# The fourth chunk's second layer of batches 1 to 6 as seven block products, with the weight sums on GpSimd

## The chip, the cores and the metric

The kernel runs on one core of a Trainium2 chip. The metric is device time in microseconds (us) of one execution. Engine names: PE is the matrix engine, DVE the vector engine, ACT the scalar engine, POOL is GpSimd. In the lines shown, `ps` is PSUM, the memory in which PE's products land and which DVE and ACT empty (an eviction); the other tiles named here lie in SBUF. The granted clock is the share of its full rate that PE was given. Times below are medians of unprofiled runs; spans, waits and instruction times come from one profiled run of each kernel.

## The reference

Eight batches of 2496 rows by 256 columns. Each is Fourier-transformed along its rows, mixed by a complex weight, soft-thresholded, and transformed back. The result goes through one of eight experts, chosen by the batch's mean: a first layer 256 to 1024 with ReLU, and a second layer 1024 to 256.

```python
X = np.fft.rfft(x, axis=1)
Yr = Xr @ w_r - Xi @ w_i + b_r
Yi = Xr @ w_i + Xi @ w_r + b_i
Yr = np.sign(Yr) * np.maximum(np.abs(Yr) - lam, 0.0)   # the same for Yi
y = np.fft.irfft(Y, n=x.shape[1], axis=1)
# experts, x being y from here on:
e_idx = np.argmax(logits, axis=1)
h = np.maximum(x[mask] @ w1[e], 0.0)
out[mask] = gate_w[mask, None, None] * (h @ w2[e])
```

## The kernel before

A Python list scheduler places every operation: each is declared with an engine, an assumed duration, a wanted time, its dependencies and the buffers it allocates and releases. Batch b's expert work is interleaved with batch b+1's transforms (towards its end, with the first of batch b+2's), so that PE always has something to do. The transforms come in groups (q). The code below is of one group. The soft threshold is a clip on DVE (`cl`) followed by four subtractions `Y = z - cl`, each with both inputs in SBUF; the inverse transform on PE waits for them.

```python
def cl_(_, cell=cell):
    nc.vector.tensor_scalar(out=cell["cl"], in0=cell["z"], scalar1=-LAM, scalar2=LAM,
                            op0=ALU.max, op1=ALU.min)
...
def y_(_, cell=cell):
    for r in range(2):
        for i in range(2):
            s = slice(64 * i, 64 * i + 64)
            nc.vector.tensor_sub(out=Y[64 * r : 64 * r + 64, :, i],
                                 in0=cell["z"][s, r], in1=cell["cl"][s, r])
...
m = S.mm([256] * n, mmv, vt, deps=[oy, t_in[4 * q + 3]], ...)   # inverse, needs Y
```

The second layer of a chunk of 512 rows normally takes eight groups of four matmuls of 256 columns. In the last batch its first four chunks use seven products of half-size blocks instead of eight, a fast form in the manner of Strassen and Winograd. It needs sums of weight blocks (tile `T`, one buffer, four subtractions of 512 elements) and sums of activations (tile `S`). A batch's `T` can be written only when the previous holder's products have released it.

```python
FAST = {(B - 1, c) for c in range(4)}
...
def add_weight_sums(b, w, wk, v):
    tk = S.tok("T", 1)                       # one buffer
    def ts(_):
        ...
        sub = nc.vector.tensor_sub
        sub(out=T[:, 0], in0=w2[:, 0, 1], in1=w2[:, 0, 0])
        ...                                  # T1, T2, T3
    t = S.op("DVE", 1.4, ts, v, deps=[w], lat=1.5, allocs=[tk])
...
# in add_fast
p5 = prod(2.4, ("F", 1), "S1", T(0), False, [o1, t_op], after=p2)
...
t_tok.rel += [p4, p5, p6, p7]                # T is free after these
```

## Time and profile before

| | before |
|---|---|
| time, 3 runs | 431.3 us (431.11 to 431.45) |
| span of the profiled run | 429.5 us |
| second-layer matmuls (L1438), product matmuls (L1252) | 1056, 224 |
| from one batch's second-layer weight load to the next | 49.97 us |
| mean granted PE clock | 1.000 |

The period is (350.02 - 200.12)/3, from the starts of the loads in GpSimd's timeline. The prediction below shows the head of the page and PE's timeline. The lines here are those that the result has to be held against. First, from the slices of the page, the PE clock that was granted, one digit for each fortieth of the span (9 is 90% or more):

```profile
PEclk9999999999999999999999999999999999999999
```

The clock is never cut.

### The profile page before, as it was taken

What the parts mean: (1) busy time and instruction counts of PE and PEld (TensorE: products, weight loads), DVE (VectorE), ACT (ScalarE), POOL (GpSimd) and SP (SyncE); (2) the same over time, 40 slices, a digit from 0 to 9 for tenths busy, and PEclk for the clock granted to TensorE, in tenths of its full rate; (3) what the DMA queues carried; (4) which work ended last, traced back from release to release, by engine and by line L of the source; (5) the groups of instructions that cost most, each with busy time, mean ns of one, the idle gap of its engine ahead of it and who ended that gap; (6) DMA issues with size and microseconds to landing.
All of it is one profiled execution on the core that took longest, in us unless ns stands there. A gap on an engine that the chain in (4) does not pass through costs nothing.

```text
span 429.5 us, 9604 instructions
## 1 busy us (share of the span) xinstructions
PE 417.4 (97%) x3601; PEld 315.9 (74%) x3601; DVE 305.3 (71%) x635; ACT 336.1 (78%) x654; POOL 60.6 (14%) x104
## 2 busy tenths in 40 slices
PE   5988999999999999999999999999999999999996
PEld 2557777887777877778677876778777787777775
DVE  1697865777777797787967787677977878414561
ACT  3789888787967887779866798678877788778884
POOL 5553100001003020033000320031200030001000
PEclk9999999999999999999999999999999999999999
DMA  7999797929885996889885998959978276521222
GB/s 151 234 172 163 129 279 238 216 75 181 230 270 106 232 186 195 251 171 203 191 247 194 197 203 209 283 117 218 194 220 253 86 166 126 181 91 56 65 99 92
DMA packets 71847, 76.98 MB, mean 179 GB/s; under 512 B 7128, under 2 KB 45744, under 8 KB 71800
## 3 DMA queue, kind: packets, MB, share of 16 engines
q1 hardware_dynamic: 58834, 56.23, 44.7%
q0 software_dynamic: 12704, 19.88, 29.1%
q8 instruction: 28, 0.46, 0.4%
q10 hardware_dynamic: 262, 0.25, 0.2%
q14 instruction: 19, 0.16, 0.1%
HBM read 57.54 MB, written 37.49 MB: 221 GB/s over the span
## 4 chain that ended last, share of the span: by engine, by line
PE 92%; DVE 3%; DMA 2%; ACT 2%; POOL 1%; issue 1%; SPq 0%; DVEq 0%; POOLq 0%
PE ps L1389 31%; PE ps L1438 27%; PE ps L914 9%; PE ps L718 4%; PE ps L547 4%; PE ps L812 3%; PE ps L1058 3%; PE ps L1252 3%; PE ps L876 3%; PE ps L1323 2%; DMA xin<-in_x_dram 1%; PE ps L751 1%; PE ps L754 1%; DMA ysb<-in_w_i_dram 1%; DVE z L766 1%; ACT ysb L1074 1%
## 5 line engine op out<-in xcount | busy, mean ns | idle before, releaser
L1402 ACT ACTIVATE hs<-ps 128x512 f16<-128x512 f32 (+3 forms) x313 | 172.1, 568 | 65.3 <-PE ps L1389 61.3
L1389 PE MATMUL ps<-ysb,w1s 128*128 128x512 f16 (+3 forms) x688 | 182.6, 359 | 0.1
L1438 PE MATMUL ps<-w2s,hs 128*128 128x256 f16 x1056 | 150.9, 272 | 0.0
L1438 PEld LDWEIGHTS <-hs 128*128 128x128 f16 x1056 | 102.0, 98 | 38.3 <-issue 0.9
L1389 PEld LDWEIGHTS <-w1s 128*128 128x128 f16 x688 | 73.9, 113 | 17.9 <-issue 0.7
L956 DVE TENSOR_TENSOR Y<-z,cl 64x512 f16<-64x512 f16 x120 | 50.4, 420 | 2.7
L928 DVE TENSOR_TENSOR tt<-ps,bias 128x512 f16<-128x512 f32 x60 | 38.6, 686 | 18.1 <-PE ps L914 17.9
L914 PE MATMUL ps<-w,XT 128*128 128x256 f16 x360 | 49.9, 273 | 0.1
L914 PEld LDWEIGHTS <-XT 128*128 128x128 f16 x360 | 34.9, 98 | 9.9 <-DVE XT L895 0.6
L1455 ACT ACTIVATE ost<-ps,gbc 128x512 f32<-128x512 f32 (+1 forms) x57 | 38.4, 675 | 2.7 <-PE ps L1438 1.9
L937 DVE TENSOR_TENSOR z<-ps,tt 128x512 f16<-128x512 f32 x60 | 38.7, 683 | 0.2
L1074 DVE CAST ysb<-ps 128x468 f16<-128x468 f32 (+1 forms) x37 | 21.4, 587 | 22.7 <-PE ps L1058 20.0
L554 ACT CAST V<-ps 128x512 f16<-128x512 f32 x52 | 30.2, 598 | 0.6
L822 ACT CAST A<-ps 120x512 f16<-120x512 f32 x46 | 26.0, 613 | 3.1 <-PE ps L812 3.1
L884 ACT CAST XT<-ps 128x512 f16<-128x512 f32 x41 | 24.3, 596 | 0.0
L1074 ACT CAST ysb<-ps 128x468 f16<-128x468 f32 (+1 forms) x47 | 21.8, 533 | 2.4 <-PE ps L1058 2.4
L1150 POOL DMA_DIRECT2D w1s<-in_moe_w_dram x8 | 6.0, 755 | 122.3 <-PE ps L1058 111.6
L547 PE MATMUL ps<-Y,ti 128*128 128x256 f16 x140 | 23.0, 272 | 0.0
L884 DVE CAST XT<-ps 128x512 f16<-128x512 f32 x19 | 13.1, 689 | 13.8 <-PE ps L876 13.0
L812 PE MATMUL ps<-xin,wa 117*120 117x512 f16 x66 | 22.8, 380 | 0.1
L1404 DVE TENSOR_SCALAR hs<-ps 128x512 f16<-128x512 f32 (+3 forms) x31 | 17.4, 568 | 7.3 <-PE ps L1389 6.5
L1058 PE MATMUL ps<-wi,V 120*128 120x117 f16 (+1 forms) x308 | 22.5, 213 | 0.0
(112 smaller groups left out, 476.5 us busy)
## 6 DMA issues: line engine op xcount, KB each, us to landing
out_dram<-ost SPq DMA_DIRECT2D x71, 256.0 KB
scr<-V SPq DMA_DIRECT2D x35, 256.0 KB
xin<-in_x_dram POOLq DMA_DIRECT2D x21, 390.0 KB, 9.8
XB<-fwd SPq DMA_DIRECT2D x30, 256.0 KB
V<-scr SPq DMA_DIRECT2D x14, 504.0 KB
fwd<-A SPq DMA_DIRECT2D x18, 360.0 KB
w1s<-in_moe_w_dram POOLq DMA_DIRECT2D x8, 512.0 KB, 7.1
w2s<-in_moe_w_dram POOLq DMA_DIRECT2D x8, 512.0 KB, 8.1
```

The costliest lines, as they stand in the source:

```text
L547: nc.tensor.matmul(pv[:, D * i : D * i + D], ti[:, 4 * q + k, :], cell["Y"](k))
L812: nc.tensor.matmul(pa[0:120, :], wa, xin_t[b][:, xcol(2 * gp) : xcol(2 * gp) + 2 * D])
L884: COPY[eng](out=cell["X"][:, ch, :, 0:2].rearrange("p a r i k -> p a i r k"), in_=hc["p"].rearrange("p (a i r k) -> p a i r k", a=2, i=2, ...
L914: nc.tensor.matmul(pm[:, D * a : D * a + D], cell["X"][:, ch, a, t].rearrange("p i k -> p (i k)"), w4[:, ch, t, :], start=(ch == 0), stop= ...
L928: nc.vector.tensor_add(out=cell["tt"][:, r], in0=cell["T", 2].rearrange("p (a c) -> p a c", a=2), in1=bias[:, r].unsqueeze(1).to_broadcast ...
L937: nc.vector.tensor_add(out=cell["z"][:, r], in0=cell["T", 1 - r].rearrange("p (a c) -> p a c", a=2), in1=cell["tt"][:, r])
L956: nc.vector.tensor_sub(out=Y[64 * r : 64 * r + 64, :, i], in0=cell["z"][s, r], in1=cell["cl"][s, r])
L1074: COPY[eng](out=yv[:, :, 12 * gb : 12 * gb + 3 * nf].rearrange("p a (g j) -> p a g j", j=3), in_=pi[:, 0 : 117 * nf].rearrange("p (g a j) ...
L1389: nc.tensor.matmul(ph[:, 0:nl], w1v[:, ch, fc // 4, :, fc % 4], ysb_t[b][:, ch, ns : ns + nl], start=(ch == 0), stop=(ch == 1))
L1402: nc.scalar.activation(out=o, in_=i, func=AFT.Relu)
L1438: nc.tensor.matmul(oc["p"][:, i, :], cell["hs"][:, ft, ts], w2s_t[b][:, ft, :], start=(ft == 0), stop=(ft == E - 1))
L1455: nc.scalar.activation(out=ost[:, 0:n], in_=oc["p"][:, 0:n], func=AFT.Copy, scale=gbc_t[b])
```

## The change

Its intent is to remove PE work, since PE sets the time: the fourth chunk of batches 1 to 6 also gets the seven products. Their weight sums go to GpSimd, which is mostly idle. Two smaller edits apply to all fast chunks: the first product waits for four of the eight activations only, and output rows are dealt to partitions in adjacent pairs.

```diff
-    FAST = {(B - 1, c) for c in range(4)}
+    FAST = {(B - 1, c) for c in range(4)} | {(b, c) for b in range(1, B - 1) for c in (3,)}
...
-            sub = nc.vector.tensor_sub
+            sub = (nc.gpsimd if b < B - 1 else nc.vector).tensor_sub
...
-        t = S.op("DVE", 1.4, ts, v, deps=[w], lat=1.5, allocs=[tk])
+        p = b < B - 1
+        t = S.op("POOL" if p else "DVE", 4.5 if p else 1.4, ts, v, deps=[w],
+                 lat=4.7 if p else 1.5, allocs=[tk])
...
-        A = {"11": lambda f, t: cell["hs"][:, f, m * t : m * t + m],
+        A = {"11": lambda f, t: cell["hs"][:, f, t:th:2],
...  (the other six operands alike)
-        p1 = prod(0, ("E", 0), "11", w2(0, 0), True, h_ops, [ek])
+        p1 = prod(0, ("E", 0), "11", w2(0, 0), True, h_ops[:4], [ek])
...
-                        "(i p) c -> p i c", p=m),
+                        "(p i) c -> p i c", i=2),
```

More of the change, by code (lines that the diff above doesn't have):

```diff
@@ L1234, in add_fast @@
         o4 = s_op("s4", 0, s4, vt(0.3), [o2])
-        A = {"11": lambda f, t: cell["hs"][:, f, m * t : m * t + m],
-             "12": lambda f, t: cell["hs"][:, 4 + f, m * t : m * t + m],
-             "22": lambda f, t: cell["hs"][:, 4 + f, th + m * t : th + m * t + m],
-             "S3": lambda f, t: cell["hs"][:, f, th + m * t : th + m * t + m],
-             "S1": lambda f, t: fc["S"][:, 0, f, m * t : m * t + m],
-             "S2": lambda f, t: fc["S"][:, 1, f, m * t : m * t + m],
-             "S4": lambda f, t: fc["S"][:, 2, f, m * t : m * t + m]}
+        A = {"11": lambda f, t: cell["hs"][:, f, t:th:2],
+             "12": lambda f, t: cell["hs"][:, 4 + f, t:th:2],
+             "22": lambda f, t: cell["hs"][:, 4 + f, th + t : nl : 2],
+             "S3": lambda f, t: cell["hs"][:, f, th + t : nl : 2],
+             "S1": lambda f, t: fc["S"][:, 0, f, t:th:2],
+             "S2": lambda f, t: fc["S"][:, 1, f, t:th:2],
+             "S4": lambda f, t: fc["S"][:, 2, f, t:th:2]}
         w2 = lambda k, h: lambda f: w2s_t[b][:, 4 * k + f, P * h : P * h + P]
```

## The prediction

> **What bounds the kernel now.** I read the head of the page first, then the chain that ended last.
>
> ```profile
> span 429.5 us, 9604 instructions
> PE 417.4 (97%) x3601; PEld 315.9 (74%) x3601; DVE 305.3 (71%) x635; ACT 336.1 (78%) x654; POOL 60.6 (14%) x104
> ...
> PE 92%; DVE 3%; DMA 2%; ACT 2%; POOL 1%; issue 1%; SPq 0%; DVEq 0%; POOLq 0%
> ```
>
> The matrix engine (PE) is busy 97% of the span, and the chain runs through it for 92%. In the list of waits, PE's own add up to under 9 us, all of them in the start-up. So a microsecond of PE work removed in the middle is a microsecond off the end, unless another engine becomes late. Busy does not mean full rate, so next come the start times of consecutive PE groups, first in the middle of the kernel (second layer L1438, first layer L1389), then in the last batch, which already uses seven products (L1252):
>
> ```profile
> 221.46 0.60 PE L1438 MATMUL ps<-w2s,hs 128*128 128x256 f16 x4
> 221.89 0.59 PE L1389 MATMUL ps<-ysb,w1s 128*128 128x512 f16 x2
> 222.33 0.60 PE L1438 MATMUL ps<-w2s,hs 128*128 128x256 f16 x4
> ...
> 404.59 0.61 PE L1252 MATMUL ps<-T,S 128*128 128x128 f16 x8
> 405.03 0.59 PE L1389 MATMUL ps<-ysb,w1s 128*128 128x512 f16 x2
> 405.46 0.61 PE L1252 MATMUL ps<-T,S 128*128 128x128 f16 x8
> ```
>
> The first column is the start. Four matmuls of 256 columns take 0.435 us of issue time (109 ns each), two of 512 take 0.435, and one block product (8 of 128 columns) takes 0.44 us (55 ns each). Weight loads (98 ns each in the groups) lie beside the matmuls and do not limit either. Multiplying the period's matmuls by these spacings (first layer 16.8 us, second 17.0, the six transform groups 15.7) gives about 49.5 us, and a batch takes 49.5 to 50: the stream has hardly a hole, no more than about 0.4 us a batch.
>
> The two engines that empty PSUM have room on average. Stretches of one batch (columns: length, PE, PE weight loads, DVE, ACT, POOL):
>
> ```profile
> 219.00:229.00 10.00, 10.00 (x81) 7.46 (x79) 7.26 (x14) 6.07 (x12) 0.00 (x0) 1.00 0.89 270
> 229.00:239.00 10.00, 10.00 (x85) 7.62 (x83) 7.98 (x22) 6.97 (x14) 3.77 (x7) 1.00 0.51 133
> 239.00:249.00 10.00, 10.00 (x112) 8.57 (x110) 8.36 (x16) 8.31 (x17) 0.80 (x2) 1.00 1.07 210
> 249.00:259.00 10.00, 10.00 (x82) 7.29 (x80) 8.15 (x16) 8.40 (x19) 3.03 (x5) 1.00 1.04 203
> ```
>
> The fourth chunk's second layer is issued at 236.7 to 243.8 us here, so its new work falls where DVE and ACT are already at 8.4 and 8.3 of 10.
>
> **What the Trainium skill says.** (1) "TensorE: Matmul & The Clock Gate", Back-to-back issue gap: it gives about 81 ns per matmul for sustained weight-load and matmul pairs of 128 columns, and 56 ns as the isolated gap. By the first figure seven products would cost 56 x 81 = 4.5 us (an estimate from that page), more than the eight they replace. The trace disagrees: 55 ns, each with its own weight load. I use the trace. (2) "GPSIMD Engine Reference", section 3.1: a two-input elementwise operation costs GpSimd about 2.6 cycles an element, twice DVE. The kernel before has no such instruction on GpSimd; its one-input operations of 128x512 took 0.78 and 1.50 us, against 0.29 us on DVE, which does not contradict it. (3) "SBUF — State Buffer", Who interferes with whom: a DVE instruction with two SBUF inputs and a GpSimd instruction that reads SBUF exclude each other for their whole length. No part of the trace before overlaps the two, so it cannot confirm this. (4) "VectorE: DVE Perf Modes", the perf-mode tier table: two-input 16-bit operations run at two elements a cycle, from PSUM at one. The trace agrees: the sums of 1024 fp16 elements took 684 to 692 ns, the additions of 512 fp32 from PSUM 683 ns.
>
> **The change part by part.**
>
> PE, per batch 1 to 6. Removed: 32 matmuls of 256 columns, 8 groups of four at 0.435 us, 3.48 us. Added: 56 of 128 columns, 7 products at 0.44 to 0.447 us (the chain has three in a row in 1.34 us), 3.08 to 3.13 us. Saved 0.35 to 0.40, say 0.38 us. All of it is on the path. Six batches: 2.3 us.
>
> DVE and ACT, per batch. Added on DVE: four sums of activations, 4 x 0.685 = 2.74 us, and three scaled additions of 256 columns at 0.482, 1.45 us. Added on either: four scaled copies of 256 columns, 4 x 0.483 = 1.93 on ACT. Removed from either: two evictions of 512 columns, 2 x 0.686 = 1.37. Net +4.75 us on the pair, whose load is 78.2 of 2 x 50 us, so 83 of 99 afterwards. Beside PE on average. Locally it is tight: from 236 to 250 us the pair is busy 10.5 + 11.5 = 22.0 of 28 us, and with 4.75 more it is 26.7, 95%.
>
> GpSimd, per batch 1 to 6: four subtractions of 512 elements. With 2.6 cycles at 1.2 GHz each is 1.1 us plus dispatch, so 1.2 to 1.5 us and 5 to 6 us in all (an estimate from the GPSIMD page and the 1.50 us row). GpSimd is 14% busy. The sums are needed a long way into a batch (the third product of the fourth chunk), while the weights land some 8 us after their issue at about 250 us, far ahead. The one tile for the sums is held until the previous batch's fourth chunk is done, so I expect them to run just after it, around the next weight issue: off the path. During those 5 to 6 us the two-SBUF-input DVE work (2.1 us per transform group of about 10 us) can be blocked, at a guess two instructions by 0.6 us, about 1 us of DVE time.
>
> Last batch: its four chunks already use the products. The first product may start after four instead of eight activations, but PE is gapless there (chunk starts follow first-layer groups with no hole), so I give it 0 to 0.2 us. Output rows become adjacent pairs, which makes longer runs per store; stores are not on the path there (DMA share 0.26), and the final piece of the kernel is still the unchanged fifth chunk. 0.
>
> Sum: 431.3 - 2.3 - 0.1 = 428.9 us if nothing becomes late.
>
> **The rivals.**
>
> A, evictions become late. In the fast form both accumulator banks are held for the whole chunk, and one half bank passes through four copies: product, copy, product, copy. Each turn is 0.44 us of product, about 0.5 of copy and the queue of ACT, so PE needs other work between the products; at 95% local load of DVE and ACT this work itself may wait for a bank. Against: in the last batch ACT takes just these copies and PE has no hole; and before, PE waits for nobody after the start, with transforms of the next batch as filler. The transform data has slack: the loads that hold GpSimd's next input load are complete at 235.2, the inverse that uses such data starts at 244.2. For: the casts at 244.6 to 249.0 must end before the next batch's first layer at 249.96, about 1 us of slack. If PE loses 0.2 us a batch, the result is 428.9 + 1.2 = 430.1; if 0.6 us, 432.5.
>
> B, GpSimd. If the sums block DVE's turn at a bad moment or push the loads of inputs and weights on the same queue, each costs up to about 1 us. For: they lie beside the same crowded stretch. Against: the weight load is a full batch ahead. It would make 429.5 to 432.
>
> C, the products run at the page's 81 ns. Then each batch loses 4.5 - 3.48 = 1.0 us, 437 us in all. The last batch's own trace speaks against it.
>
> D, the whole static order is remade by the kernel's list scheduler, so small holes can come or go anywhere: some +-0.7 us.
>
> **Range and chances.** Full gain 428.9; I charge 0.15 us a batch, 0.9 us, for A and B together, as the local load is near saturation: 429.8 us. The low end is the full gain with a favourable reordering, 428.3; the high end has PE losing about 0.5 us a batch, 432.0. Faster by over 2% means below 422.7, beyond anything that 2.3 us of removed PE time can give: 0.01. Slower by over 2% means above 439.9, for which C and A would have to meet: 0.015. Within 2%: 0.975.
>
> **What would show it.** Right: matmuls at L1438 fall from 1056 to 864 and those of the product line rise from 224 to 560, with product spacing near 0.44 us in batches 1 to 6; PE's waits stay near zero after the start; ACT and DVE together gain about 28 us; four GpSimd subtractions per batch of 1.2 to 1.5 us each, with the next weight load following without delay. A wrong size of the gain would show in products at over 0.46 us. Rival A would show as idle PE before first-layer or product matmuls released by ACT or DVE at the end of each batch, rival B as two-input DVE rows well over 0.42 us beside GpSimd's. The prediction fails if those holes exceed 0.5 us a batch, or if the reordering moves the transforms of the next batch so that the first layer waits at a batch's start.

## More of the kernel before

```profile
244.20 0.37 PE L1058 MATMUL ps<-wi,V 120*128 120x117 f16 x4
244.41 0.60 PE L547 MATMUL ps<-Y,ti 128*128 128x256 f16 x4
...
248.11 0.83 PE L1323 MATMUL ps<-hs,w2s 128*128 128x192 f16 x8
```

The subtractions end at 244.23. The inverse (L547) follows its predecessor on PE 0.21 us after that one's start, with no wait marked in brackets. It starts only 0.18 us after Y is complete: Y has next to no slack in this order.

The costliest-groups view (count, then busy us and mean ns, then idle us before them): the 120 threshold subtractions take 420 ns each.

```profile
L956 DVE TENSOR_TENSOR Y<-z,cl 64x512 f16<-64x512 f16 x120 | 50.4, 420 | 2.7
```

Then DVE's and PE's timelines of the same group of a batch (start, busy us, engine, line, operation, count):

```profile
242.49 1.74 DVE L956 TENSOR_TENSOR Y<-z,cl 64x512 f16<-64x512 f16 x4
```

## The result

| | before | after |
|---|---|---|
| time, 4 runs each | 431.38 us (431.11 to 431.87) | 453.55 us (452.11 to 455.02) |
| span of the profiled run | 429.5 us | 450.7 us |
| product / second-layer matmuls | 224 / 1056 | 560 / 864 |
| mean granted PE clock | 1.000 | 0.985 |

The ratio is 1.0513, with a 95% interval of 1.0468 to 1.0558: 5% slower. A ratio here is the mean time of one kernel's fast runs over that of the other's of the same rounds, so not quite the ratio of the medians quoted.

Head, slices and chain of the changed kernel's page:

```profile
span 450.7 us, 9985 instructions
...
PE 422.8 (94%) x3745; PEld 320.9 (71%) x3745; DVE 334.3 (74%) x664; ACT 341.9 (76%) x679; POOL 90.7 (20%) x128
...
PEclk9999999999999899998999989999999989999999
...
PE 84%; DVE 9%; DMA 2%; issue 2%; ACT 1%; POOL 0%; DVEq 0%; SPq 0%; POOLq 0%
```

PE's share of the chain fell from 92 to 84%, DVE's rose from 3 to 9%, and four slices have a lowered clock. PE is busy longer although it has less to do. The list of waits (us in total, times, longest) names what it waits for, and what starts GpSimd's sums:

```profile
POOL T L1193 <- PE ps L1254: 64.9, 5, 40.2
...
PE ps L547 <- DVE Y L956: 14.9, 10, 2.0
```

This second wait did not exist before. The group in question, with the same 120 instructions:

```profile
L956 DVE TENSOR_TENSOR Y<-z,cl 64x512 f16<-64x512 f16 x120 | 67.4, 561 | 2.7
```

The mean of 561 ns hides two kinds. Five times, four instructions take 1.28 us each and the others 0.42. One of the five, on GpSimd, DVE and PE:

```profile
253.65 1.34 POOL L1193 TENSOR_TENSOR T<-w2s 128x512 f16<-128x512 f16 x1 [5.23 <-PE ps L1254]
...
257.54 1.32 POOL L1196 TENSOR_TENSOR T<-w2s,T 128x512 f16<-128x512 f16 x1
```

```profile
254.01 5.13 DVE L956 TENSOR_TENSOR Y<-z,cl 64x512 f16<-64x512 f16 x4
```

```profile
255.57 0.37 PE L1058 MATMUL ps<-wi,V 120*128 120x117 f16 x4
257.90 0.27 PE L547 MATMUL ps<-Y,ti 128*128 128x256 f16 x1 [1.96 <-DVE Y L956]
259.19 0.49 PE L547 MATMUL ps<-Y,ti 128*128 128x256 f16 x3 [1.02 <-DVE Y L956]
...
260.91 1.45 PE L1325 MATMUL ps<-hs,w2s 128*128 128x192 f16 x8
```

The sums of batch b start as soon as the products of batch b-1 release `T`. Within 0.4 us DVE begins the threshold of batch b+1. Four GpSimd subtractions and four DVE subtractions run over the same 5.2 us, and each DVE one takes 1.28 us, about as long as a GpSimd one, instead of 0.42. PE runs out of other work and waits 1.96 us and then 1.02 us for Y. And after it has its data, eight matmuls at L1325 take 1.45 us where before they took 0.83. The windows view (columns: stretch, length, PE, PE weight loads, DVE, ACT, POOL, clock, DMA share, GB/s) shows why:

```profile
255.00:260.00 5.00, 2.02 (x22) 1.59 (x21) 4.91 (x6) 0.83 (x3) 4.52 (x4) 1.00 0.27 74
260.00:265.00 5.00, 5.00 (x45) 4.42 (x43) 1.76 (x5) 3.58 (x9) 0.63 (x1) 0.66 0.90 138
```

PE is busy 2.0 of 5 us in the first window, and in the next the clock granted is 0.66. That is a mean over 5 us: in windows of 1 us the clock is 0.50 from 260.40 to 263.81 and 1.00 around it. This happened after four of the five waits, each time for 3.41 us, so each cost 1.7 us.

The traces also show why not after the fifth. The four cuts start at 151.17, 205.78, 260.40 and 366.21 us, which is 16, 16 and 31 times 3.413 us apart, as if the clock were decided on a fixed grid of that step. Divide the trace by this grid and add up, cell by cell, the time in which PE issued nothing: it is 2.10 to 3.01 of 3.41 us in the cells just before the four cuts, and at most 1.96 in the cells of the wait that no cut followed. All ten cuts within PE's work in the profiled runs last 3.41 us and follow a cell with 2.10 us or more (sums_after_y: 2.28 to 2.58); of the cells from 40 us on that no cut follows, one has as much (2.10, sums_after_ysb). That is a rule worked out from these traces alone, and no run was made to test it. By it, the same two waits cost 1.7 us of clock or nothing, depending on where in the grid they fall.

**Where 21.2 us of span went.** The waits are 14.9. The wait counted is a little shorter than the hole: the group at 255.57 needs 0.21 us to issue (its like before: 244.20 to 244.41), so PE issued nothing for 257.90 - 255.78 = 2.12 us, 0.16 more than counted. Ten such: 1.6. The clock: (1 - 0.985) x 450.7 = 6.8, which is also four times 1.7. (The other three runs had clocks of 0.979 to 0.983, so they may have lost up to some 9.5 us.) Less 2.3 for the products: 14.9 + 1.6 + 6.8 - 2.3 = 21.0.

### The profile page after: what moved, and what is told of

Its sections match the earlier page's. It is cut to its first block, busy times and chain, and to the rows that moved or that the text cites. A ratio compares the mean times of both kernels' runs of the same rounds, so it can differ in the third digit from the quotient of the medians.

```text
span 450.7 us, 9985 instructions
## 1 busy us (share of the span) xinstructions
PE 422.8 (94%) x3745; PEld 320.9 (71%) x3745; DVE 334.3 (74%) x664; ACT 341.9 (76%) x679; POOL 90.7 (20%) x128
## 4 chain that ended last, share of the span: by engine, by line
PE 84%; DVE 9%; DMA 2%; issue 2%; ACT 1%; POOL 0%; DVEq 0%; SPq 0%; POOLq 0%
PE ps L1391 29%; PE ps L1440 20%; PE ps L914 9%; PE ps L1254 5%; DVE Y L956 5%; PE ps L547 4%; PE ps L718 4%; PE ps L812 3%; PE ps L1058 3%; PE ps L876 3%; PE ps L1325 2%; DMA xin<-in_x_dram 1%; DVE z L937 1%; PE ps L751 1%; PE ps L754 1%
## 5 line engine op out<-in xcount | busy, mean ns | idle before, releaser
L1404 ACT ACTIVATE hs<-ps 128x512 f16<-128x512 f32 (+3 forms) x317 | 177.5, 580 | 52.6 <-PE ps L1391 49.7
L1440 PE MATMUL ps<-w2s,hs 128*128 128x256 f16 x864 | 123.4, 273 | 0.0
L1440 PEld LDWEIGHTS <-hs 128*128 128x128 f16 x864 | 83.7, 98 | 30.9 <-issue 0.9
L956 DVE TENSOR_TENSOR Y<-z,cl 64x512 f16<-64x512 f16 x120 | 67.4, 561 | 2.7
L1074 ACT CAST ysb<-ps 128x468 f16<-128x468 f32 (+1 forms) x63 | 33.5, 564 | 9.7 <-PE ps L1058 9.6
L554 ACT CAST V<-ps 128x512 f16<-128x512 f32 x47 | 27.8, 601 | 16.8 <-PE ps L547 16.3
L547 PE MATMUL ps<-Y,ti 128*128 128x256 f16 x140 | 24.1, 275 | 14.9 <-DVE Y L956 14.9
L1457 ACT ACTIVATE ost<-ps,gbc 128x512 f32<-128x512 f32 (+1 forms) x45 | 30.2, 672 | 3.0 <-PE ps L1440 1.9
L547 PEld LDWEIGHTS <-ti 128*128 128x128 f16 x140 | 13.2, 98 | 22.0 <-issue 16.4
L1058 PE MATMUL ps<-wi,V 120*128 120x117 f16 (+1 forms) x308 | 26.6, 225 | 0.0
L1254 PEld LDWEIGHTS <-hs 128*128 128x128 f16 x320 | 20.9, 98 | 6.3 <-ACT ost L1269 1.2
L1058 PEld LDWEIGHTS <-V 120*128 120x128 f16 x308 | 22.1, 104 | 2.8
```

Of the source, the lines that this page charges most:

```text
L547: nc.tensor.matmul(pv[:, D * i : D * i + D], ti[:, 4 * q + k, :], cell["Y"](k))
L956: nc.vector.tensor_sub(out=Y[64 * r : 64 * r + 64, :, i], in0=cell["z"][s, r], in1=cell["cl"][s, r])
L1058: nc.tensor.matmul(pi[:, 117 * i : 117 * i + M], V2[:, g, ch * P : ch * P + P], w)
L1074: COPY[eng](out=yv[:, :, 12 * gb : 12 * gb + 3 * nf].rearrange("p a (g j) -> p a g j", j=3), in_=pi[:, 0 : 117 * nf].rearrange("p (g a j) ...
L1254: nc.tensor.matmul(fc[dst[0]][0:m, dst[1], t, :], A[a](f, t), bb(f), start=start and t == 0 and f == 0, stop=f == 3, skip_group_check=True)
L1404: nc.scalar.activation(out=o, in_=i, func=AFT.Relu)
```

## The experiments

**Theory H (hold).** GpSimd's subtractions hold DVE's two-input subtractions back, instruction by instruction; PE waits for Y; its idleness lowers the clock. **Rivals:** A, the evictions are late, or the remade order is at fault (D); or GpSimd, being busy, delays the loads that it issues; or the row and first-product edits cost something; or the waits and the clock are independent, the clock being cut for another reason. Unless told otherwise, a kernel's result was correct, and its edit is against the changed kernel. "Order kept" means that each engine's instruction order is as in the changed kernel. The expectations call H "theory L", A and D together "rival S" (or S2), and the delayed loads "rival P".

### The sums without reads

GpSimd fills `T` with zeros instead of subtracting: same place and order, no SBUF input. The result is wrong, as in m2_half and m0_later.

```diff
-            sub(out=T[:, 0], in0=w2[:, 0, 1], in1=w2[:, 0, 0])
+            nc.gpsimd.memset(T[:, 0:2], 0.0) if b < B - 1 else sub(out=T[:, 0], in0=w2[:, 0, 1], in1=w2[:, 0, 0])
...  (the other three alike, on 2:4, 0:2 and 2:4)
```

> Wrong result on purpose: the four subtractions on GpSimd of batches 1 to 6 become four zero fills of twice as many elements, so that GpSimd is about as long at work in the same places (about 1.2 us each) but reads nothing. The order on PE, DVE, ACT and the DMA queue is unchanged, row for row. Theory L (DVE's subtractions with two SBUF inputs wait for GpSimd's, PE waits for DVE, and PE's clock is cut after that wait): the Y subtractions are back at 0.42 us, PE waits for none of them, clock 1.00, 428.5 to 430.5 us. Rival S (the remade order or the chain of copies in the fast chunk costs the time): stays above 445. Rival P (GpSimd's occupancy delays its weight loads): stays above 445 too, since GpSimd is as busy.

Measured 434.85 us (433.31 to 436.47), ratio 1.0076. Y was back at 0.42 us, and no wait for L956 was left: the subtractions cause the hold, and neither the order, which was kept, nor the evictions, nor GpSimd's being busy. That it is their reading, and not something else in which a subtraction differs from a fill, is argued and not shown: no run had GpSimd read in another way. But the time was 5.6 us above the full gain, for a reason I had not thought of. Fills need no weights, so batch 1's ran at 52 us already, where the changed kernel's sums still wait for the weight load (they run at 60.9). There DVE was due to do another kind of instruction, the clip of a threshold (L779), which has one input:

```profile
51.87 4.53 DVE L779 TENSOR_SCALAR cl<-z 128x1024 f16<-128x1024 f16 x1
```

```profile
55.14 0.98 POOL L1196 MEMSET T<- 128x1024 f16 x1
```

```profile
57.18 0.39 PE L547 MATMUL ps<-Y,ti 128*128 128x256 f16 x2 [3.86 <-DVE Y L781]
```

The clip took 4.53 us; the kernel before has it at 0.43. It ended only after the last of the four fills, which ran back to back from 52.47 to 56.12. PE waited 3.86 us, and the clock fell again (0.50 for 3.41 us, 1.7 us lost). So the experiment had brought a hold of its own, once. The next one leaves batch 1 as it is (its sums meet nothing in the changed kernel, at 1.15 to 1.16 us each):

```diff
-            ... if b < B - 1 else sub(...)
+            ... if 1 < b < B - 1 else sub(...)
```

> Wrong result on purpose: as the run with zero fills, but batch 1 keeps its real subtractions, since there the fills met DVE's clip of 1024 elements (4.53 us instead of 0.47) and PE waited 3.9 us; zero fills only in batches 2 to 6. The order is that of the changed kernel. Theory L: nothing holds DVE now, no wait of PE after the start, clock 1.00, a batch takes 49.5 us instead of 50.0; 428.6 to 429.6 us, which is the gain that the seven products were forecast to bring. Rival S2 (a part of the loss is not the exclusion but comes with the remade order): 431 us or more.

Measured 429.83 us (428.94 to 430.07), ratio 0.9959 (0.9946 to 0.9973), clock 1.000, no wait for Y. A batch takes 49.55 us against 49.97 before. That is 0.42 us gained by the products in each batch, and all 22 us of the loss gone, by replacing only five batches' sums with fills.

### Half of the sums

The first two subtractions real, the last two fills.

> Wrong result on purpose: the first two subtractions on GpSimd stay, the last two become zero fills of about the same length; the order everywhere is that of the changed kernel. Theory L: two of the four Y subtractions of one transform group per batch are held by about 0.87 us each instead of four, so DVE is 1.7 us late instead of 3.4, PE waits about 1.3 us a batch instead of 3.0; with five batches 6.5 us plus a smaller loss of clock: 435 to 444 us. Rivals S and P: no change, above 450.

```diff
-            sub(out=T[:, 2], in0=w2[:, 1, 1], in1=w2[:, 0, 1])
-            sub(out=T[:, 3], in0=w2[:, 1, 0], in1=T[:, 1])
+            nc.gpsimd.memset(T[:, 2:4], 0.0) if b < B - 1 else sub(...)   # twice
```

Measured 437.07 us (436.75 to 437.82), ratio 1.0131, clock 1.000.

```profile
PE ps L547 <- DVE Y L956: 6.5, 10, 1.1
```

The waits are dosed by the number of reading instructions: two holds fewer take (14.9 - 6.5)/5 = 1.7 us of counted wait from each batch, which is two times 1.28 - 0.42. And waits of 1.10 and 0.19 us leave the clock at 1.000: PE issued nothing for at most 1.62 us in any stretch of 3.41.

### The clock by itself

Nine matmuls on constant data fill the first wait of PE, without changing Y or the sums. If the clock is cut because PE idles, it comes back; if not, nothing changes.

```diff
-                                   if wide else bank(tv))
+                                   if wide else bank(tv)); [nc.tensor.matmul(pv, warm[:, 0:P], warm) for _ in range(9 if b > 2 and q == 1 and u == 0 else 0)]
```

> Right result: the changed kernel with nine dummy matmuls of 512 columns (1.94 us) put before the inverse product that waits for the held Y, in the five batches where it waits; they go into the bank which that product overwrites. All else is in the same order. Theory: the exclusion costs the wait (about 3.0 us a batch, which stays, 1.96 of it now filled), and the cut clock afterwards (6.8 us in the profiled run) comes from PE having stood idle: clock 1.00 and 446 to 448 us, and less spread between runs. If the cut clock has another cause: 452 to 456 us and clock 0.98.

Measured 445.93 us (445.68 to 446.96), ratio 1.0343, a little better than expected. While PE works the clock is 1.000; the 0.998 comes from a cut after PE's last matmul (440.8 us), which costs nothing.

```profile
252.87 2.11 PE L544 MATMUL ps<-warm 128*128 128x512 f16 x9
255.00 0.27 PE L547 MATMUL ps<-Y,ti 128*128 128x256 f16 x1
256.29 0.49 PE L547 MATMUL ps<-Y,ti 128*128 128x256 f16 x3 [1.02 <-DVE Y L956]
```

The useless matmuls gained 7.6 us over the changed kernel. Y still took 562 ns in the mean, and the second wait of 1.02 us stayed. So the clock's share is a consequence of PE's idleness, and real. The 7.6 us, a difference of medians, are not the clock alone: five holes fewer, at 0.16 us of issue each, make 0.8 of them. The rest agrees with the 6.8 read from the trace.

### The other parts of the change

First the sums back on DVE (the order is remade), then none of the products, only the first product's half and the row pairs in the last batch.

```diff
-            sub = (nc.gpsimd if b < B - 1 else nc.vector).tensor_sub
+            sub = nc.vector.tensor_sub
-        p = b < B - 1
+        p = False
```

> Right result: the weight sums of batches 1 to 6 go to DVE, as those of the last batch do; all else as changed (the list scheduler remakes the order). Theory L: the seven products gain their 2.3 us, DVE takes 1.7 us more a batch: 428.5 to 431 us, no wait of PE after the start, clock 1.00. Rival S: above 440, as the fast chunk and its chain of copies are all there.

Measured 432.25 us (431.68 to 433.24), ratio 1.0016 (1.0003 to 1.003), somewhat above what I had expected. Y was back at 419 ns and the clock at 1.000. But PE had new small waits, the largest of them for scaled additions on DVE (1.5 us in four) and for activations (0.7 in three). The holes eat the gain: rival A or D, which this run cannot tell apart, exists at some 3 us in this form, though not as the cause of the 22.

```diff
-    FAST = {(B - 1, c) for c in range(4)} | {(b, c) for b in range(1, B - 1) for c in (3,)}
+    FAST = {(B - 1, c) for c in range(4)}
```

> Right result: only the small parts of the change (first product after four activations, alternate rows per tile and so paired output rows) in the last batch; batches 1 to 6 as before, no sums on GpSimd. All theories: within 0.5 us of before, 430.9 to 431.8 us.

Measured 431.38 us (431.21 to 432.1), ratio 1.0002 (0.9989 to 1.0016): worth nothing, as predicted.

With the sums on DVE, I also tried the products in the second or the third chunk, where DVE and ACT might have more room:

```diff
-    FAST = ... for c in (3,)}
+    FAST = ... for c in (1,)}          # dve_chunk2; (2,) in dve_chunk3
```

> Right result: weight sums on DVE, and the seven products in the second chunk of batches 1 to 6 instead of the fourth, where before DVE and ACT were busy 7.3 and 6.1 of 10 us. If what the sums-on-DVE kernel lost was the local load of DVE and ACT in the fourth chunk: 428.8 to 430.8 us. If the fast chunk's own chain of copies costs PE the same anywhere: 431.5 to 433 us.

> Right result: the same with the third chunk. Local load theory: 429 to 431.3 us, between the second and the fourth chunk. Chain of copies: 431.5 to 433 us.

Measured 431.1 us (430.58 to 431.89), ratio 0.9991 (0.9965 to 1.0018), and 430.76 us (430.44 to 431.21), ratio 0.9981 (0.9956 to 1.0007). Neither is told apart from before: both intervals hold 1. In the second chunk PE had a hole of 0.3 us ahead of the last of the seven products in each batch. Placing the sums on DVE is safe but gives the gain back in small holes.

### Moving the sums in time

If the collision is one of time, sums on GpSimd that come after Y must keep the gain. Two tries through the scheduler:

```diff
-        t_tok.rel += [p4, p5, p6, p7]
+        t_tok.rel += [p4, p5, p6, p7, a12]     # sums_after_y
```

```diff
-        ... ts, v, deps=[w],
+        ... ts, v, deps=[w] + y_ops,           # sums_after_ysb
```

> Right result: the tile of weight sums is released one step later, after the last scaled addition of the fast chunk, which stands behind the four Y subtractions in DVE's queue, so GpSimd's subtractions come after them and meet DVE's copies from PSUM instead. The list scheduler remakes parts of the order. Theory L: the Y subtractions take 0.42 us, PE does not wait for them: 428.6 to 431 us. If the exclusion also holds for copies from PSUM or the subtractions meet another two-input DVE operation: 433 to 445 us.

> Right result: GpSimd's sums wait until the batch's own input (ysb) is complete, about 8 us later than in the changed kernel, beside the sums of transformed halves (L895) and the next group's chain. Theory L: better than the changed kernel, but a two-input DVE operation or two a batch can still be held by up to 1.3 us each, where PE follows closely behind: 429 to 436 us.

Both missed. The first gave 448.09 us (447.62 to 450.68), ratio 1.0404, the second 445.5 (444.34 to 446.45), ratio 1.0327. In each the scheduler's remade order let the sums meet Y all the same. Of the first:

```profile
249.75 1.15 POOL L1193 TENSOR_TENSOR T<-w2s 128x512 f16<-128x512 f16 x1 [4.26 <-PE ps L1254]
```

```profile
251.33 2.56 DVE L956 TENSOR_TENSOR Y<-z,cl 64x512 f16<-64x512 f16 x2
```

The addition that I had made the release wait for came before Y in the new order. The first sum now ran alone (1.15 us, its time unheld), the later ones met Y, whose four took 4.30 us (the line shows the first two; the view ended there). PE waited 10.7 us for Y in the first run (three cuts of the clock) and 8.1 in the second (two cuts). These are failed shifts, not evidence against H: the time follows the holes (table below).

The third try makes GpSimd read one element of Y first, a dependency that cannot be reordered:

```diff
+            if 1 < b < B - 1:
+                nc.gpsimd.tensor_copy(out=T[64:65, 0, 0, 0:1],
+                                      in_=Y_of[b + 1, 1][64:65, 1, 1, 0:1])
             sub(out=T[:, 0], in0=w2[:, 0, 1], in1=w2[:, 0, 0])
...  (and the sums' dependency on that Y, declared to the scheduler)
```

> Right result: GpSimd first copies one element of the Y that the changed kernel's sums collided with (batch after, second group), so its subtractions really start only after that Y is complete; the scheduler is told of this dependency and remakes parts of the order. Theory L: Y subtractions at 0.42 us, and the next stretch of DVE is copies from PSUM: 428.6 to 431 us, if the remade order brings no other collision; a further two-input group met by the sums would show as 1.28 us rows and 435 to 445 us.

Measured 431.13 us (430.25 to 431.42), ratio 0.9983 (0.9963 to 1.0003). In its profile Y takes 420 ns, the sums 1.15 to 1.16 us each, and PE no longer waits for Y: 22 us are gone. What is missing to the full gain is some 2 us. The remade order left only small holes, which together come to that (table below), and a later sum met another two-input DVE instruction (L896, 0.76 us instead of 0.42).

### Shorter instructions in the same place

Each subtraction is split into four of 128 elements (order kept). If the hold lasts for one GpSimd instruction, a DVE instruction should wait for a short one only.

```diff
-            sub(out=T[:, 0], in0=w2[:, 0, 1], in1=w2[:, 0, 0])
+            [sub(out=T[:, 0, i], in0=w2[:, 0, 1, i], in1=w2[:, 0, 0, i]) for i in range(4)] if 1 < b < B - 1 else sub(...)
...  (the other three alike)
```

> Right result: in batches 2 to 6 each of the four subtractions on GpSimd is cut into four of 128 elements, all else in the order of the changed kernel. Theory L, in the form that DVE's two-input subtraction waits until one whole GpSimd instruction is done: each of the four Y subtractions is held by a quarter as much or somewhat more for the fixed part (0.2 to 0.4 us instead of 0.86), DVE is 0.8 to 1.6 us late, PE waits 0.3 to 1.2 us a batch, no cut clock: 431 to 436 us. If instead GpSimd keeps the shared side for as long as its work in a row lasts, cutting it changes nothing: 452 to 456 us.

Measured 431.0 us (430.72 to 431.17), ratio 0.9985 (0.9966 to 1.0004).

```profile
244.15 2.23 DVE L956 TENSOR_TENSOR Y<-z,cl 64x512 f16<-64x512 f16 x4
```

```profile
PE ps L547 <- DVE Y L956: 1.2, 5, 0.2
```

The sums run just beside Y as before, GpSimd works longer on them (7.1 us, from 243.79 to 250.91), and yet Y's four take 2.23 us instead of 5.13. The hold follows the length of the GpSimd instruction, not that of the work in a row, and splitting the holder takes nine tenths of PE's waits for Y away.

### A version that beats both

m0_later had shown that fills do not hold Y. So fills may serve as a delay ahead of the real sums, order kept: they write what the sums overwrite. Three of them (2.71 us) first, then two:

```diff
+            [nc.gpsimd.memset(t, 0.0) for t in (T[:, 0:2], T[:, 2:4], T[:, 3])] if 1 < b < B - 1 else 0;   # fill_first
+            [nc.gpsimd.memset(t, 0.0) for t in (T[:, 0:2], T[:, 2:4])] if 1 < b < B - 1 else 0;            # fill_shorter
             sub(out=T[:, 0], in0=w2[:, 0, 1], in1=w2[:, 0, 0])
```

> Right result: in batches 2 to 6 GpSimd first fills the tile of sums with zeros (2560 elements in three instructions, about 2.7 us, which hold no two-input DVE instruction), then does the four real subtractions unchanged. PE, DVE, ACT and DMA queue keep the order of the changed kernel; the subtractions only come about 2.7 us later, after the Y subtractions. Theory L (the overlap in time is the whole loss): Y at 0.42 us, no wait of PE for it, 428.8 to 430.2 us, some 0.4% under before. If the real reads of the weights cost something wherever they lie, or push the weight loads: 431.5 to 440 us.

Measured 431.74 us (431.07 to 432.27), ratio 1.0004: a miss. Y was free, but the sums now ended so late that the last one met the next two-input DVE instruction, a sum of the forward transform:

```profile
251.23 1.16 POOL L1196 TENSOR_TENSOR T<-w2s,T 128x512 f16<-128x512 f16 x1
```

```profile
251.73 0.94 DVE L895 TENSOR_TENSOR XT<-XT 128x512 f16<-128x512 f16 x1
```

It took 0.94 us instead of 0.42, and PE then waited 0.4 us in each of four batches for the DVE evictions behind it. With two fills the sums sit between Y and that instruction:

> Right result: as fill_first without the third fill of 512 elements, so the real subtractions come about 2.2 us later than in the changed kernel instead of 2.7 us. In fill_first the Y subtractions were free, but the last of GpSimd's subtractions met the sum of transformed halves (0.94 us instead of 0.42), and PE waited 0.40 us a batch for what follows it. Theory L: with 0.5 us less, the four subtractions fit between Y and that sum: both at 0.42 us, the 0.4 us a batch are back: 429.0 to 430.3 us, below before. If a real read costs something wherever it lies: 431 to 432 us as with fill_first.

```profile
243.76 2.13 POOL L1193 MEMSET T<- 128x1024 f16 x2 [4.06 <-PE ps L1254]
...
249.44 1.16 POOL L1196 TENSOR_TENSOR T<-w2s,T 128x512 f16<-128x512 f16 x1
```

```profile
244.15 1.74 DVE L956 TENSOR_TENSOR Y<-z,cl 64x512 f16<-64x512 f16 x4
...
250.49 0.40 DVE L895 TENSOR_TENSOR XT<-XT 128x512 f16<-128x512 f16 x1
```

Measured 429.45 us (428.73 to 429.9), ratio 0.9947 (0.9929 to 0.9964), correct, as expected. It is the fastest correct kernel, by half a per cent over before. Its batch takes 49.49 us (350.24 - 201.78, over 3) against 49.97.

### The account over all runs

One sum ties these runs together: the time before in the same call, less 2.3 for the products, plus PE's holes over those of the kernel before, plus what the clock cost while PE worked. A hole is the time between two matmul starts beyond the spacing of an unbroken run (55 ns for 128 columns, 109 for 256, 217 for 512, double in a cut), added up in the trace from 40 us to the last matmul; the kernel before has 3.3 us of them. A cut costs 1.71 us. The clock on record is not used for this: its mean can include a cut after PE's last matmul, as in fill_shorter (0.998, where no cut falls in PE's work).

| kernel | waits for the threshold (times) | holes over before | clock | sum | measured |
|---|---|---|---|---|---|
| after | 14.9 (10) | 16.7 | 6.8 | 452.6 | 453.55 |
| m2_half | 6.5 (10) | 7.9 | 0 | 437.2 | 437.07 |
| m0_memset | 3.9 (1) | 3.9 | 1.7 | 434.9 | 434.85 |
| warm_fill | 5.1 (5) | 7.7, and 9.8 of dummy matmuls | 0 | 446.4 | 445.93 |
| sums_after_y | 10.7 (10) | 14.2 | 5.1 | 448.3 | 448.09 |
| sums_after_ysb | 8.1 (8) | 13.6 | 3.4 | 445.9 | 445.5 |
| split_16 | 1.2 (5) | 1.9 | 0 | 431.1 | 431.0 |
| m0_later | 0 | 1.0 | 0 | 429.9 | 429.83 |
| fill_shorter | 0 | 1.3 | 0 | 430.5 | 429.45 |
| fill_first | 0 | 3.2 | 0 | 432.1 | 431.74 |
| sums_wait_y | 0 | 2.0 | 0 | 431.2 | 431.13 |
| sums_dve | 0 | 4.3 | 0 | 433.5 | 432.25 |
| dve_chunk2 | 0 | 2.5 | 0 | 431.7 | 431.1 |
| dve_chunk3 | 0 | 2.1 | 0 | 431.3 | 430.76 |

(The dummies: five times nine of 512 columns at 0.217 us.) The holes are of one profiled run, the measured times are medians. The largest misses are 1.3 us (sums_dve, whose profiled run took 433.24), 1.1 (fill_shorter) and 1.0 (the changed kernel, whose profiled run took 452.35). So what the kernels with remade orders are short of is many small holes on PE.

## Why the prediction was wrong

It said 429.8 us, with a range of 428.3 to 432.0; the result was 453.55.

- **PE's saving was right.** 0.38 us a batch was predicted, the batch became 0.42 to 0.48 us shorter wherever the hold was absent (m0_later, fill_shorter), and these two kernels are 1.8 and 2.3 us faster than the one before (ratios 0.9959 and 0.9947), where 2.4 was forecast if nothing became late. That m0_later's median meets the predicted 429.8 is chance: 0.9 us of that number was a charge for delays. The matmul counts fell and rose exactly as foretold. Rival C (products at 81 ns) is refuted by this.
- **The last batch's edits were right**: nothing (rest_only).
- **GpSimd's durations were nearly right**: 1.15 us unheld, 1.21 to 1.34 beside DVE, where 1.2 to 1.5 was estimated.
- **The step that failed is the GpSimd paragraph and rival B, in size and place.** The prediction wrote of the blocked work "at a guess two instructions by 0.6 us, about 1 us of DVE time", and called the sums "off the path". Measured: four instructions by 0.86 us, 3.4 us of DVE time in each of five batches. The mechanism and even the moment were named: the sums would run "just after" the previous batch's fourth chunk. Even the sign to look for was named: two-input DVE rows "well over 0.42 us beside GpSimd's". What was not done was to look which DVE instructions stand at that moment. It was the threshold of the next batch, four two-input instructions in a row, whose reader on PE follows 0.18 us later in the trace before. Of 3.4 us of held DVE time PE waited 2.98 (14.9/5). The reasoning about averages, with DVE at 8 of 10, could not show this; one line of DVE's timeline against one of PE's could.
- **A term was missing altogether**: a waiting PE can lose its clock. It cost 6.8 us by the trace, on top of the waits, and warm_fill, which filled most of the idleness, got that back.
- **Rival A, or D, was real but small**: some 3 us in sums_dve, where the sums add to DVE and the order is remade, against the 0.15 us a batch charged for A and B together. In the changed kernel's own order it is not visible: with the hold gone, nearly the whole gain appears.
- **One sign was missed**: ACT and DVE together were to gain about 28 us. They gained 34.8, but 17.0 of that is the hold; in m0_later, without it, they gained 16.4 (the pages' busy times). The count of new instructions was as forecast (29 + 25 = 54), so the sum of single durations was too high a measure of the load: DVE's records overlap (three sums of 0.68 us start 0.60 us apart). It did not decide the result.

What stays open: sums_wait_y and the DVE variants keep only part of the gain because of small holes on PE, and these have no single cause. Their orders were remade, and the holes differ from one to the next.

## What to carry to other kernels

Before moving work to an engine that is "mostly idle", find what makes that work ready, and look in the timeline at what every other engine does in just those microseconds; busy shares do not show it. If the two kinds of instruction exclude each other, split the holder into short instructions or shift it by a real dependency or a harmless delay, and check the next instruction that it may meet. Where the bounding engine is PE, a new wait should be counted with the clock that it may lose afterwards: here 1.7 us or nothing for the same waits.

## What the Trainium skill lacked or had wrong

- "SBUF — State Buffer", Who interferes with whom: confirmed in kind. Two-input DVE subtractions were held by reading GpSimd instructions (1.28 against 0.42 us) and not by fills (four fills over the threshold in m0_later: 1.74 us for four, as before). The page does not say how a run of instructions on each side shares the lock. Two-input DVE instructions each waited about one GpSimd instruction (4 x 1.28 = 5.13 us beside four sums), while a single clip beside four fills came through only after all four (4.53 us). The cost was one-sided here: GpSimd's sums grew from 1.15 to 1.21 to 1.34 us, DVE's threefold. Nor did they exclude each other for their whole recorded lengths: the eight together took 5.21 us (253.65 to 258.86), while four of 1.15 and four of 0.42 make 6.3. Why is left open by the page and by the traces.
- "TensorE: Matmul & The Clock Gate", HAM oscillation: the page's rule is to have no PE gap above about 3.4 us. Here two waits of 1.96 and 1.02 us, with one matmul between them, were followed by a clock of 0.50 for 3.41 us in four of five cases, 1.7 us lost each time. Shorter idleness than the rule's was enough: 2.10 us and more, not in one piece, within one cell of a grid of 3.413 us (a cell with 1.96 us was followed by no cut, and one with 2.10 neither). A window of that length the page has, but no figure for how much of it must be idle. Waits of 1.10 and 0.19 us lowered nothing (m2_half).
- The same page, Back-to-back issue gap: 81 ns for each sustained pair of weight load and 128-column matmul. The products run at 55 ns, 336 more of them in the changed kernel than before, and the gain predicted from 55 ns was measured.
